# A scan, an FFN and a mixture of experts on one core: the scan's products of a chunk in one TensorE group, and PSUM split three, three and two

## The chip, the cores and the metric

One core of a Trainium2 chip runs the whole kernel. The metric is device time in microseconds (us): the median of three runs before is 608.58 us (608.17 to 608.62).

## The reference

Three stages follow one another. First a linear recurrence over 4 sequences of 768 tokens, 8 heads of 32 columns with a state of 16 (`_attn_ref`); the kernel takes it in chunks of 128 tokens. Its output, 3072 tokens of 256 columns, goes through a feed-forward layer whose activation is a rational function (`_moe_ref`), and that through a top-1 mixture of 8 experts (`_moe2_ref`).

```python
# first stage, per chunk
y_intra = einsum('bhij,bhjd->bhid', (C @ B^T) * L, x)       # L: decays, causal
y_inter = einsum('bhin,bhnd->bhid', C, state) * decay_to_i
state = decay_full * state + sum(B * x * decay_from_j)
# second stage
h = x @ w_in                                                # 256 -> 2048
g = (a0 + a1*h + a2*h^2 + a3*h^3) / (1 + |b0|*|h| + |b1|*h^2 + 1e-6)
x = g @ w_out                                               # 2048 -> 256
# third stage, for the tokens of each expert e
xn = x / (norm(x) + 1e-6);  logits = xn @ en.T / tau;  e = argmax(logits)
out = max(softmax(logits)) * (relu(x @ w1[e]) @ w2[e])      # 256 -> 1024 -> 256
```

## The kernel before

The kernel is recorded as operations with a due time `at`, an engine, a cost and the tiles that each reads and writes. `Plan.run` lists them by these: on a free engine it starts the ready operation of the earliest due time for whose new tiles there are buffers. The list fixes the order of instructions on every engine; on the chip each engine works through its list in that order and waits by semaphores.

The 3072 tokens are 24 chunks of 128 and 6 *units* of 512 (numbered 0 to 5). Work that is in the trace at the same time:

- **First stage** (`s1_chunk`, L635 to L723). For each chunk: `c` (L666), two score products, one for each half of the heads, in float32, each into a bank of its own; ScalarE and GpSimd, or VectorE, mask them into `m` (L672, L675, L680). `st` (L688): the chunk's addition to the state, which VectorE adds up in `sx` (L695, L697). `y` (L706 and L712): the outputs, made from the state before the chunk and from `m`, one operation for each half; ScalarE and VectorE copy them out as a high and a low part, `x1h` (L722) and `x1l` (L723). These four operations have due times of their own, so TensorE's list puts other work between them. The chunks of unit u+1 are made while unit u is in the second stage.
- **Second stage** (`block`, L729 to L765). Each unit has 16 blocks of 128 columns. A block's first product `h` (L738, six matmuls of 512 columns) goes to a bank of the pool `ps_h`. Five ScalarE instructions (L743, L744, L745, L749, L750), four VectorE instructions (L747, L752, L753, L754) and one GpSimd instruction (L755) work out the activation as a high and a low part, `gh` and `gl`; L754, which writes `p`, is the last that reads the bank. The second product (L764, six matmuls) adds into the two banks `acc`.
- **Routing** (`route`): after a unit the tokens are transposed with their logits (`tk`, L799, L801) and scattered to expert lists in device memory (L858).
- **Third stage**. Three short passes (`first_pass`: products `fh`, `fy`) run while the last unit ends; passes of 2 to 4 tiles of 128 tokens follow (`run_pass`). A pass loads its tokens `g` (L961), transposes them (`t`, L969), splits them into `xh` and `xl` (L972, L975), and makes the products `eh` (L1023) and `y` (L1032). `gate` (L978 to L1009) works out each token's softmax weight by a row of small instructions of VectorE and ScalarE, all on SBUF tiles. `deliver` scales the result (L1046, L1048), and GpSimd scatters it (L1052) by the token numbers in the last column of `g`.

PSUM has 8 banks. Before, 4 are in `ps_h` (for `h`, `eh`, `fh` and, at the start, weight conversions), 2 in `ps_a` (`acc`, and the third stage's `y`), 2 in `ps_s` (all that `bank()` makes: `c`, `st`, `y`, `tk`, `t` and others):

```python
H_B = 4        # banks in ps_h
S_B = 2        # banks in ps_s
```

Of the kernel before, what the change touches and what calls it, by code (L numbers as in the profile page):

```python
# [47 lines left out]
H_B = 4  # L48

DIRECT = 2  # L50
S_B = 2
# [224 lines left out]
def ssm_ffn_moe_kernel(  # L276
# [29 lines left out]
    def dve(n, k=0):  # L306
        return 0.069 + n / 960 + 0.06 * k
# [122 lines left out]
    tri, ones = keep([P, P], BF16, "tri"), keep([P, P], BF16, "ones")  # L430
    io, tok, cw8, ke, kmin = keep([P, NE], I32, "io"), keep([P, NCH], I32, "tok"), keep([P, NE], F32, "cw8"), keep([P, NE], BF16, "ke"), keep([P, NE], F32, "kmin")
# [204 lines left out]
    def s1_chunk(u, j, at, ph):  # L636
# [23 lines left out]
        ms_ = [plan.val(s1p, [P, 4, P], F32, f"m{q}{n}", "m", 3) for q in range(2)]  # L660

        def f():
# [4 lines left out]
        op("PE", 1.28, at, f, r=[t["bc"], cz], w=cs)  # L667
# [14 lines left out]
        so = state.get("s")  # L682
        if not last:
            st = bank(f"st{n}")

            def f():
                for q in range(2):
                    T.matmul(out=st[64 * q:64 * q + 64, 0:P], lhsT=bw[:, q].rearrange("p n r -> p (n r)"), rhs=t["xt"]()[:, j, q * P:(q + 1) * P], start=True, stop=True)  # L688
            op("PE", 0.3, at + ph, f, r=[bw, t["xb"]], w=[st])
            sn = sx[c_ % SX]  # L690
            for q in range(2):
                def f(q=q):
                    qs = slice(64 * q, 64 * q + 64)
                    if first:
                        V.tensor_copy(out=sn[qs, q], in_=st[qs, 0:P])  # L695
                    else:
                        V.scalar_tensor_tensor(out=sn[qs, q], in0=so[qs, q], scalar=ec[qs, 1, (j + 1) * P - 1:(j + 1) * P], in1=st[qs, 0:P], op0=ALU.mult, op1=ALU.add)  # L697
                op("DVE", dve(P, 1), at + ph + 0.3, f, r=[st] + ([] if first else [ec, (so, q)]), w=[(sn, q)])
            state["s"] = sn
        y = bank(f"y{n}")  # L700

        def f(q):
            o = slice(q * P, (q + 1) * P)
            if not first:
                for r in range(4):
                    T.matmul(  # L706
                        out=y[r * HD:(r + 1) * HD, o], lhsT=so[:, q, r * HD:(r + 1) * HD], rhs=cz[:, r, cl],
                        start=True, stop=False, skip_group_check=True, tile_position=(0, r * HD),
                    )
            for r in range(4):  # L710
                h = 4 * q + r
                T.matmul(  # L712
                    out=y[r * HD:(r + 1) * HD, o], lhsT=t["xt"]()[:, j, h * HD:(h + 1) * HD], rhs=ms_[q][:, r, :],
                    start=first, stop=True, skip_group_check=True, tile_position=(0, r * HD),
                )
        for q in range(2):
            op(
                "PE", 0.3 if first else 0.5, at + (2 + q) * ph, lambda q=q: f(q),
                r=[ms_[q], t["xb"]] + ([] if first else [cz, so]), w=[(y, q)],
            )  # L720
        yv = lambda: y[:, 0:256].rearrange("p (k t) -> p k t", k=2)
        op("ACT", act(256), at + 3 * ph + 0.7, lambda: A.activation(out=x1h[:, :, xl], in_=yv(), func=AF.Copy), r=[y], w=[(x1h, jx)])  # L722
        op("DVE", dve(256), at + 3 * ph + 0.9, lambda: V.tensor_tensor(out=x1l[:, :, xl], in0=yv(), in1=x1h[:, :, xl].bitcast(F32), op=ALU.subtract), r=[y, (x1h, jx)], w=[(x1l, jx)])  # L723
# [231 lines left out]
    def tokens(e, t0, n, at):  # L955
# [6 lines left out]
        for t in range(n):  # L962
            tr = bank(f"t3_{nm}_{t}")
            o = slice(t * P, (t + 1) * P)
# [517 lines left out]
```

## Time and profile before

| | us |
| --- | --- |
| median of 3 runs | 608.58 |
| the profiled execution | 609.72 |
| its span in the profile | 607.9 |
| TensorE busy | 555.0 (91%) |
| VectorE busy | 478.7 (79%) |
| ScalarE busy | 467.1 (77%) |
| GpSimd busy | 249.7 (41%) |

The shares are means over stages with different limits. In the times of the trace, units 0 to 5 of the second stage begin at 41, 103, 165, 228, 286 and 350 us; the last ends at 418 us, and the passes after the short ones run from 459 to 595 us. A busy TensorE is modelled from the matmuls' starts; where it shows no idle time, it may still lose time between groups of matmuls, which is read from their starts.

### The profile page before, as it was taken

What the parts mean: (1) busy time and instruction counts of PE and PEld (TensorE: products, weight loads), DVE (VectorE), ACT (ScalarE), POOL (GpSimd) and SP (SyncE); (2) the same over time, 40 slices, a digit from 0 to 9 for tenths busy, and PEclk for the clock granted to TensorE, in tenths of its full rate; (3) what the DMA queues carried; (4) which work ended last, traced back from release to release, by engine and by line L of the source; (5) the groups of instructions that cost most, each with busy time, mean ns of one, the idle gap of its engine ahead of it and who ended that gap; (6) DMA issues with size and microseconds to landing.
All of it is one profiled execution on the core that took longest, in us unless ns stands there. A gap on an engine that the chain in (4) does not pass through costs nothing.

```text
span 607.9 us, 10415 instructions
## 1 busy us (share of the span) xinstructions
PE 555.0 (91%) x3429; PEld 430.0 (71%) x3429; DVE 478.7 (79%) x989; ACT 467.1 (77%) x941; POOL 249.7 (41%) x233
## 2 busy tenths in 40 slices
PE   1667989999999999999999999899998979999991
PEld 0244657776667666767676787677888979999991
DVE  7997899989888798899997889884456667767430
ACT  6898989999998899989997998893256667557330
POOL 2573334446444444454445434433433543222111
PEclk9997999999999999999999999999999989999996
DMA  7960515113102120110010001681266855544000
GB/s 245 390 206 18 160 30 160 45 55 97 45 0 84 51 61 19 54 62 18 2 46 27 1 2 54 219 286 36 89 193 174 238 154 177 173 142 153 18 23 14
DMA packets 47919, 61.08 MB, mean 100 GB/s; under 512 B 4135, under 2 KB 37776, under 8 KB 47856
## 3 DMA queue, kind: packets, MB, share of 16 engines
q1 hardware_dynamic: 45360, 53.92, 29.0%
q0 software_dynamic: 2496, 6.41, 2.9%
q8 instruction: 29, 0.48, 0.4%
q14 instruction: 34, 0.28, 0.1%
HBM read 46.11 MB, written 14.72 MB: 100 GB/s over the span
## 4 chain that ended last, share of the span: by engine, by line
PE 59%; issue 8%; DMA 7%; DVE 7%; ACT 4%; POOL 3%; SPq 1%; another core or an unknown queue 0%; POOLq 0%; ACTq 0%
PE h L738 19%; PE acc L764 19%; PE eh L1023 4%; PE y L1032 4%; PE c L666 3%; DMA g<-xs 2%; PE y L706 2%; PE y L712 2%; DMA ra<-in_w 2%; POOL out_dram L1052 1%; PE tk L801 1%; PE fy L1119 1%; DMA out_dram<-yo,g 1%; DMA fa<-in_w 1%; DVE gh L752 1%
## 5 line engine op out<-in xcount | busy, mean ns | idle before, releaser
L755 POOL TENSOR_TENSOR gl<-p,v 128x512 fp32r<-128x512 f32 x96 | 127.4, 1329 | 176.0 <-DVE p L754 76.1
L738 PE MATMUL h<-x1h,wiw 128*128 128x512 f32 x384 | 142.0, 413 | 7.5 <-DVE p L754 5.2
L764 PE MATMUL acc<-gh,wow 128*128 128x512 f32 x384 | 112.0, 413 | 0.0
L738 PEld LDWEIGHTS h<-x1h,wiw 128*128 128x128 f32 x384 | 73.5, 192 | 34.0 <-issue 7.6
L764 PEld LDWEIGHTS acc<-gh,wow 128*128 128x128 f32 x384 | 68.0, 188 | 29.6 <-issue 15.9
L752 DVE SCALAR_TENSOR_TENSOR gh<-h,as,v 128x512 fp32r<-128x512 f32 x96 | 71.7, 747 | 14.1 <-ACT v L750 13.5
L753 DVE SCALAR_TENSOR_TENSOR u<-u,lq,gh 128x512 f32<-128x512 f32 x96 | 78.9, 822 | 0.8
L747 DVE SCALAR_TENSOR_TENSOR h<-p,sl,h 128x512 f32<-128x512 f32 x96 | 71.9, 749 | 6.7 <-ACT v L744 6.4
L738 PE MATMUL h<-x1l,wiw 128*128 128x512 f32 x192 | 76.8, 400 | 0.0
L743 ACT ACTIVATE p<-h,kk 128x512 f32<-128x512 f32 x96 | 65.3, 680 | 11.8 <-POOL gl L755 6.1
L754 DVE SCALAR_TENSOR_TENSOR p<-h,as,u 128x512 f32<-128x512 f32 x96 | 71.6, 745 | 3.0 <-DVE bw L651 0.2
L745 ACT ACTIVATE u<-v,qb 128x512 f32<-128x512 f32 x96 | 69.5, 724 | 1.5
L749 ACT ACTIVATE v<-u,lq 128x512 f32<-128x512 f32 x96 | 69.4, 722 | 1.6
L750 ACT ACTIVATE v<-v 128x512 f32<-128x512 f32 x96 | 60.4, 630 | 1.0
L764 PE MATMUL acc<-gl,wow 128*128 128x512 f32 x192 | 60.6, 396 | 0.1
L744 ACT ACTIVATE v<-h 128x512 f32<-128x512 f32 x96 | 56.9, 593 | 2.5 <-POOL gl L755 2.5
L1026 DVE SCALAR_TENSOR_TENSOR hl<-eh,hh 128x256 fp32r<-128x256 f32 (+1 forms) x72 | 34.2, 479 | 27.3 <-ACT hh L1025 26.8
L1025 ACT ACTIVATE hh<-eh 128x256 fp32r<-128x256 f32 (+1 forms) x72 | 30.5, 425 | 28.2 <-PE eh L1023 24.4
L1052 POOL DMA_INDIRECT out_dram<-yo,g x22 | 23.8, 1080 | 67.8 <-DVE yo L1048 34.6
L1032 PE MATMUL y<-ebh,hh 128*128 128x256 f32 x176 | 51.2, 291 | 0.3 <-ACT hh L1025 0.3
L1032 PE MATMUL y<-ebh,hl 128*128 128x256 f32 x176 | 50.5, 287 | 0.2 <-DVE hl L1026 0.2
L1032 PE MATMUL y<-ebl,hh 128*128 128x256 f32 x176 | 49.8, 283 | 0.0
(238 smaller groups left out, 1143.1 us busy)
## 6 DMA issues: line engine op xcount, KB each, us to landing
ra<-in_w SPq DMA_DIRECT2D x32, 256.0 KB
rb<-in_w SPq DMA_DIRECT2D x32, 256.0 KB
xb<-in_xb SPq DMA_DIRECT2D x12, 384.0 KB
xs<-empty SPq DMA_DIRECT2D x8, 530.0 KB
wiwr<-in_w_in SPq DMA_DIRECT2D x8, 512.0 KB
wowr<-in_w_out SPq DMA_DIRECT2D x8, 512.0 KB
xrow<-row SPq DMA_DIRECT2D x6, 530.0 KB
bc<-in_bct SPq DMA_DIRECT2D x12, 256.0 KB
```

What stands on the lines that cost most here:

```text
L738: T.matmul(out=h.t, lhsT=part(wiw[g_], z)[:, k, fs], rhs=xx[:, k, :], start=(k == 0 and e == 0), stop=(k == 1 and e == 2))
L743: op("ACT", act(512, 1), s, lambda: A.activation(out=pp.t, in_=h.t, func=AF.Square, bias=kk.t), r=[h, kk], w=[pp])
L745: op("ACT", acts(512) + 0.06, s + 0.3, lambda: A.activation(out=uu.t, in_=vv.t, func=AF.Square, bias=qb.t), r=[vv, qb], w=[uu])
L747: op("DVE", dve(512, 1), s + 0.8, lambda: stt(out=h.t, in0=pp.t, scalar=sl.t, in1=h.t, op0=ALU.add, op1=ALU.mult), r=[h, pp, sl], w=[h])
L749: op("ACT", acts(512) + 0.09, s + 0.9, lambda: A.activation(out=vv.t, in_=uu.t, func=AF.Ln, bias=lq.t), r=[uu, lq], w=[vv])
L750: op("ACT", acts(512), s + 1.0, lambda: A.activation(out=vv.t, in_=vv.t, func=AF.Exp, scale=-1.0), r=[vv], w=[vv])
L752: op("DVE", dve(512, 1), s + 1.5, lambda: stt(out=gh.t, in0=h.t, scalar=as_.t, in1=vv.t, op0=ALU.add, op1=ALU.mult), r=[h, as_, vv], w=[gh])
L753: op("DVE", dve(512, 1), s + 1.6, lambda: stt(out=uu.t, in0=uu.t, scalar=lq.t, in1=gh.t.bitcast(F32), op0=ALU.add, op1=ALU.mult), r=[uu, l ...
L754: op("DVE", dve(512, 1), s + 1.7, lambda: stt(out=pp.t, in0=h.t, scalar=as_.t, in1=uu.t, op0=ALU.add, op1=ALU.subtract), r=[h, as_, uu], w ...
L755: op("POOL", pool2(512), s + 2.1, lambda: G.tensor_tensor(out=gl.t, in0=pp.t, in1=vv.t, op=ALU.mult), r=[pp, vv], w=[gl])
L764: T.matmul(out=acc[dh].t, lhsT=part(wow[g_], z)[:, i % 2, dh * P:(dh + 1) * P], rhs=x.t, skip_group_check=True, start=(i == 0 and e == 0), ...
L1032: T.matmul(out=y[t // 2][:, t % 2 * DM:(t % 2 + 1) * DM], lhsT=hx[:, o], rhs=wb[w][:, f % 2, :], start=(f == 0 and i == 0 and t % 2 == 0), ...
```

## The change

1. `H_B` goes from 4 to 3 and `S_B` from 2 to 3.
2. From the second 512 tokens on (first-stage units of 256 tokens numbered 2 and up: chunks 4 to 23) a chunk's scores, its `st` and the *previous* chunk's `y` are one TensorE operation. `st` and the previous `y` share one bank `gy`. The last chunk of each 512 tokens has its `y` in an operation of its own behind that.
3. `tokens`: two tiles are transposed into one bank and copied out by one instruction each of ScalarE and VectorE.
4. `gate`: the maximum with 1e-36 becomes a bias of the logarithm, and, except in the first short pass, the small values stand in a bank of `ps_h` (`gp`).
5. GpSimd copies the token numbers out of `g` into `ix`, and the scatter reads that.
6. In the very last pass each of the two tiles has an output bank, and each tile's second product is an operation of its own.

```diff
-H_B = 4
+H_B = 3
-S_B = 2
+S_B = 3
...
+        together = u >= 2
+        pend = state.pop("pend", None)
+        if together:
+            both = bank(f"gy{n}")
+            st = both
...
+        if together:
+            def f():
+                scores()
+                if not last:
+                    states(256)
+                if pend:
+                    for q in range(2):
+                        pend[0](both, q)
+            op(
+                "PE", 0.95 + (0 if last else 0.2) + (0.45 if pend else 0), at, f,
+                r=[t["bc"], cz] + ([] if last else [bw, t["xb"]]) + (pend[1](0) + pend[1](1) if pend else []),
+                w=cs + ([] if last else [(both, 2)]) + ([(both, 0), (both, 1)] if pend else []),
+            )
+            if pend:
+                pend[2](both, at + 0.7)
+        else:
+            op("PE", 1.28, at, scores, r=[t["bc"], cz], w=cs)
...
+        if together and jx < BU // P - 1:
+            state["pend"] = sums, reads, outputs
+        elif together:
+            y = bank(f"y{n}")
...
-        for t in range(n):
+        for t in range(0, n, 2):
+            m = min(2, n - t)
...
-        dv(0.08, lambda: V.tensor_scalar(out=s2[:, 0:n], in0=s2[:, 0:n], scalar1=1e-36, scalar2=None, op0=ALU.max), [s2], [s2])
+        plan.op("ACT", 0.1, sh(at, -0.09, 0), lambda: A.activation(out=s(), in_=s2[:, 0:n], func=AF.Ln, bias=tiny.t), r=[s2, *tiny_], w=[S])
-        dv(0.08, lambda: V.tensor_tensor(out=rc[:, 0:n], in0=rc[:, 0:n], in1=s2[:, 0:n], op=ALU.mult), [rc, s2], [rc])
+            gp = plan.val(ps_h, [P, 512], F32, f"gp{nm}", "h", H_B, True)
+        dv(0.08, lambda: V.tensor_tensor(out=rc(), in0=rc(), in1=s2[:, 0:n], op=ALU.mult), [RC, s2], [RC])
...
+        for t in range(n):
+            op("PE", 1.4 / 4, sh(at + 0.8, 0.36, 0) + (6.0 if t == n - 1 and f > 4 else 0.0), lambda t=t: mm2([t], 1), r=[hh, hl, *wb], w=[y[t]])
...
-                    out=out, out_offset=bass.IndirectOffsetOnAxis(ap=g[:, t, ROW - 1:].bitcast(I32), axis=0), in_=yo.t, in_offset=None,
+                    out=out, out_offset=bass.IndirectOffsetOnAxis(ap=ix[:, t:t + 1], axis=0), in_=yo.t, in_offset=None,
...
+        ix = plan.val(sp, [P, TPE], I32, f"ix{nm}", "ix", 4)
+        op("POOL", 0.15, at + 2 * parts[0] - 2.0, lambda n=sum(parts): G.tensor_copy(out=ix[:, 0:n], in_=g[:, 0:n, ROW - 1].bitcast(I32)), r=[g], w=[ix])
```

The order on TensorE in unit 2, before: the products of chunk 13 (`c0_13` and `c1_13` are its scores; rows of other work are left out).

```order
L666 MATMUL c0_13_2080<-cz_6_1618,bc_6_1426 128x512
L666 MATMUL c1_13_2081<-cz_6_1618,bc_6_1426 128x512
...
L688 MATMUL st_13_2191<-xb_6_1180,bw_13_1716 64x128 x2
L738 MATMUL h_2_7_2194<-x1h4_1368,wiw3_470 128x512
...
L706 MATMUL y_13_2210<-cz_6_1618,sx0_132 32x128 x4
L712 MATMUL y_13_2210<-m0_13_2097,xb_6_1180 32x128 x4
L764 MATMUL acc2_0_2041<-gh_2_4_2146,wow2_453 128x512
...
L706 MATMUL y_13_2210<-cz_6_1618,sx0_132 32x128 x4
L712 MATMUL y_13_2210<-m1_13_2099,xb_6_1180 32x128 x4
```

And of the change, a little later: chunk 14's scores and `st`, and with them the `y` of chunk 13 (the rows that read `m0_13` and `m1_13`), follow one another with nothing between.

```order
L678 MATMUL c0_14_2229<-cz_7_1782,bc_7_1696 128x512
L678 MATMUL c1_14_2230<-cz_7_1782,bc_7_1696 128x512
L682 MATMUL gy_14_2231<-xb_7_1606,bw_14_1857 64x128 x2
L688 MATMUL gy_14_2231<-cz_6_1620,sx0_133 32x128 x4
L694 MATMUL gy_14_2231<-m0_13_2081,xb_6_1154 32x128 x4
L688 MATMUL gy_14_2231<-cz_6_1620,sx0_133 32x128 x4
L694 MATMUL gy_14_2231<-m1_13_2083,xb_6_1154 32x128 x4
```

So four groups between large products have become one. In TensorE's whole list such groups, each with large products (`h` or `acc`) on both sides, number 18, 19, 18 and 18 in units 1 to 4 before (the `tk` and `rk` of routing with them), and 9, 8, 8 and 7 now; in unit 0 they go from 15 to 8.

The order on VectorE in the third stage, before: the gate of the pass of expert rank 4 (`rc4_0`, `sq4_0`, `s24_0` are its small tiles) stands ahead of the splits `xl4_0` of that pass's tokens.

```order
L997 RECIPROCAL rc4_0_5626<-sq4_0_5596 128x3
L998 TENSOR_TENSOR rc4_0_5626<-rc4_0_5626,s24_0_5534 128x3
L999 TENSOR_TENSOR sq4_0_5596<-sq4_0_5596,rc4_0_5626 128x3
L1000 TENSOR_SCALAR sq4_0_5596<-sq4_0_5596 128x3
L1001 RECIPROCAL rc4_0_5626<-sq4_0_5596 128x3
L1026 SCALAR_TENSOR_TENSOR hl2_2_4_5647<-eh2_2_4_5613,hh2_2_4_5635 128x256
L975 TENSOR_TENSOR xl4_0_5652<-t3_4_0_0_5631,xh4_0_5644 128x2x128
```

And of the change (`gp4_0` is the bank with the small values, `hl4_0` an operand of that pass's second product).

```order
L1019 TENSOR_TENSOR xl4_0_5627<-t3_4_0_0_5597,xh4_0_5614 128x2x256
...
L1019 TENSOR_TENSOR xl4_0_5627<-t3_4_0_2_5629,xh4_0_5614 128x2x128
...
L1081 SCALAR_TENSOR_TENSOR hl4_0_5_5888<-eh4_0_5_5840,hh4_0_5_5875 128x384
L1019 TENSOR_TENSOR xl5_0_5892<-t3_5_0_0_5870,xh5_0_5890 128x2x256
L1052 RECIPROCAL gp4_0_5903<-sq4_0_5499 128x3
L1053 TENSOR_TENSOR gp4_0_5903<-gp4_0_5903,s24_0_5411 128x3
```

The gate has moved behind both splits and most of the pass, and its multiplication reads one operand from PSUM.

## Rows read from the trace of the kernel before

**Rows 1.** Windows: stretch and its length, then busy us (instructions) of each engine, granted TensorE clock, DMA share, GB/s.
```profile
41.20:103.27 62.07, 56.27 (x310) 37.77 (x311) 55.62 (x98) 56.37 (x106) 26.36 (x22) 0.95 0.28 81
103.27:165.27 62.00, 62.00 (x385) 43.55 (x384) 55.62 (x98) 58.98 (x108) 29.80 (x26) 1.00 0.27 76
103.27:349.87 246.60, 245.27 (x1491) 170.48 (x1490) 220.20 (x374) 227.65 (x408) 115.86 (x101) 1.00 0.15 45
349.87:417.70 67.83, 63.83 (x293) 50.36 (x292) 59.57 (x126) 58.26 (x118) 29.76 (x26) 1.00 0.40 129
458.57:595.24 136.67, 132.58 (x1002) 131.02 (x1000) 87.43 (x218) 77.28 (x202) 39.28 (x34) 0.99 0.45 137
480.00:500.00 20.00, 16.44 (x122) 15.88 (x121) 12.35 (x30) 11.33 (x34) 10.03 (x8) 0.91 0.65 193
```

**Rows 2.** The chain that ended last, 212 to 221 us: start, us, what it was.
```profile
213.40 1.06 PE c L666 x4
214.45 1.60 PE h L738 x6
216.06 0.37 PE st L688 x4
216.42 1.60 PE acc L764 x6
218.02 1.40 PE h L738 x6
219.42 0.35 PE y L706 x8
219.78 0.22 PE y L712 x8
```

**Rows 3.** Waits of ScalarE, 103 to 350 us: total us, times, longest.
```profile
ACT p L743 <- PE h L738: 5.5, 11, 1.0
```

**Rows 4.** Timeline of TensorE: first matmul of blocks 0 and 12, units 0 and 5.
```profile
41.20 0.77 PE L738 MATMUL h<-x1h,wiw 128*128 128x512 f32 x1 [1.81 <-ACT wow L571]
...
88.59 0.50 PE L738 MATMUL h<-x1h,wiw 128*128 128x512 f32 x1 [1.44 <-DVE p L754]
...
349.87 0.39 PE L738 MATMUL h<-x1h,wiw 128*128 128x512 f32 x1
...
389.74 0.50 PE L738 MATMUL h<-x1h,wiw 128*128 128x512 f32 x1 [0.83 <-DVE p L754]
```

**Rows 5.** Timeline of VectorE: `p` of those blocks; the third is unit 2, block 13.
```profile
53.86 0.73 DVE L754 SCALAR_TENSOR_TENSOR p<-h,as,u 128x512 f32<-128x512 f32 x1
...
100.47 0.75 DVE L754 SCALAR_TENSOR_TENSOR p<-h,as,u 128x512 f32<-128x512 f32 x1
...
226.19 0.75 DVE L754 SCALAR_TENSOR_TENSOR p<-h,as,u 128x512 f32<-128x512 f32 x1
...
357.96 0.75 DVE L754 SCALAR_TENSOR_TENSOR p<-h,as,u 128x512 f32<-128x512 f32 x1
...
403.45 0.75 DVE L754 SCALAR_TENSOR_TENSOR p<-h,as,u 128x512 f32<-128x512 f32 x1
```

**Rows 6.** Timeline of all engines, 490 to 494.5 us.
```profile
490.18 2.93 DVE L998 TENSOR_TENSOR rc<-rc,s 128x3 f32<-128x3 f32 x1
...
490.59 1.28 POOL L950 TENSOR_TENSOR eal<-ra,eah 128x512 fp32r<-128x512 f32 x1
...
491.80 1.27 POOL L950 TENSOR_TENSOR ebl<-rb,ebh 128x512 fp32r<-128x512 f32 x1
...
494.41 0.33 PE L969 MATMUL t<-ident,g 128*128 128x128 f32 x1 [3.56 <-DVE xl L975]
```

**Rows 7.** Waits of TensorE, 400 to 480 us: total us, times, longest.
```profile
PE ck L1181 <- DVE xl L975: 1.4, 1, 1.4
PE tk L799 <- ACT row L804: 1.2, 1, 1.2
```

**Rows 8.** Timeline of GpSimd, from 590 us: the last scatter.
```profile
597.32 0.97 POOL L1052 DMA_INDIRECT out_dram<-yo,g  x1 [0.30 <-issue]
```

More of the change, by code (lines that the diff above doesn't have):

```diff
@@ L660, in s1_chunk, with scores @@
         ms_ = [plan.val(s1p, [P, 4, P], F32, f"m{q}{n}", "m", 3) for q in range(2)]
-        def f():
+        so = state.get("s")
+        together = u >= 2
+        pend = state.pop("pend", None)
+        st = y = None
+        if together:
+            both = bank(f"gy{n}")
+            st = both
+        elif not last:
+            st = bank(f"st{n}")
+        def scores():
             for q in range(2):
@@ L681, in s1_chunk @@
                 op("DVE", dve(512), at + 0.3, g, r=[c, mask], w=[m])
-        so = state.get("s")
         if not last:
[L684 to L689, printed above, removed]
+            so_ = 256 if together else 0
+            if not together:
+                op("PE", 0.3, at + ph, lambda: states(0), r=[bw, t["xb"]], w=[st])
             sn = sx[c_ % SX]
@@ L699, in s1_chunk @@
+                op("DVE", dve(P, 1), at + ph + 0.3, f, r=[(st, 2) if together else st] + ([] if first else [ec, (so, q)]), w=[(sn, q)])
             state["s"] = sn
[L700 to L723, printed above, removed]
+        if together and jx < BU // P - 1:
+            state["pend"] = sums, reads, outputs
+        elif together:
+            y = bank(f"y{n}")
+            def f():
+                for q in range(2):
+                    sums(y, q)
+            op("PE", 0.75, at + 2.5 * ph, f, r=reads(0) + reads(1), w=[(y, 0), (y, 1)])
+            outputs(y, at + 3 * ph + 0.7)
+        else:
+            y = bank(f"y{n}")
+            for q in range(2):
+                op("PE", 0.3 if first else 0.5, at + (2 + q) * ph, lambda q=q: sums(y, q), r=reads(q), w=[(y, q)])
+            outputs(y, at + 3 * ph + 0.7)
@@ L1066, in run_pass @@
             nm = f"{e}_{t0 + q}"
[L1067 removed]
+            per = 1 if apart and q + n == sum(parts) else 2
+            y = [plan.val(*z, True) for z in [(ps_a, [P, 512], F32, f"y{nm}_{b}", "acc", 2) for b in range((n + per - 1) // per)]]
             for f in range(8):
[L1069 removed]
+                hidden(nm, e, q, n, f, xh, xl, y, at + f * n / 4, per == 1)
             at += 2 * n
[L1071 removed]
+            deliver(nm, q, n, ix, y, gt, at + 0.9, per)
             q += n
@@ L1098, in first_pass @@
         op("ACT", act(2 * n * P), at - 1.5, lambda: A.activation(out=x.t.rearrange("p k t -> p (k t)"), in_=tr[:, 0:2 * n * P], func=AF.Copy), r=[tr], w=[x])
-        gt = gate(plan, nm, g, n, at + 4 * step, blk)
+        gt = gate(plan, nm, g, n, at + 4 * step, blk, not small, [tiny])
+        ix = plan.val(blk, [P, 2], I32, f"fix{nm}", "fix", 3)
+        op("POOL", 0.15, at + 4 * step, lambda: G.tensor_copy(out=ix[:, 0:n], in_=g[:, 0:n, ROW - 1].bitcast(I32)), r=[g], w=[ix])
         y = bank(f"fy{nm}") if small else plan.val(ps_a, [P, 512], F32, f"fy{nm}", "acc", 2, True)
```

122 lines of the change are left out of this document (76 added, 46 removed).

## The prediction

> **What bounds the kernel now.** I read the windows by stage first. While units 1 to 4 are in the second stage (103.27 to 349.87 us) TensorE is busy for 245.27 of 246.60 us; in the passes from 458.57 us on for 132.58 of 136.67 [rows 1]. So in both stretches time is won only where TensorE has less to do, or where it no longer stands still. The reader should also see what comes next: ScalarE is busy for 227.65 us of the first stretch (92.3%), and in its densest part, unit 1, for 58.98 of 62.00 us (95.1%). VectorE stands at 220.20 us (89.3%).
>
> Busy time hides what the change is about, so I then followed the chain that ended last, which is TensorE work end to end. A large product takes 1.40 us behind another large one and 1.60 us behind one of the first stage's groups; the groups themselves take 1.06 (`c`), 0.37 (`st`) and 0.35 + 0.22 us (half of `y`) [rows 2]. A group that stands alone therefore costs its own time and 0.20 us more.
>
> Last I looked at what limits a bank of `ps_h`: from a block's first matmul to the end of its `p`. Block 13 of unit 2 starts at 218.02 in the chain and its `p` ends at 226.94, which is 8.9 us [rows 2, 5]. A block comes every 3.9 us there (62.00 / 16, [rows 1]), so three banks give 11.6 us. In units 0 and 5 it is longer: over blocks 0 to 12 of unit 0 the first takes 13.4 us and the last 12.6, with a mean of 14.1 over the 13; in unit 5 the first takes 8.8 and the last 14.5, mean 12.7 [rows 4, 5].
>
> **The change, part by part.**
>
> *One group per chunk, units 1 to 4.* The order counts 73 groups between large products before and 32 after, 41 fewer. At 0.20 us [rows 2] that is 8.2 us. Inside a merged group each product may also lose some of the start that it pays alone. No row shows one at full clock, so I bound it by nothing and by 0.25 us for each of 16 chunks (4 us), and take 0.1 us, since the rows that read `m` take only 0.22 us behind rows of the same kind against 0.35 us for the first of a pair [rows 2]. TensorE would then need 9.8 us less. Not all of that can arrive. ScalarE's 227.65 us at the 95.1% it reached in unit 1 make 239.4 us, 7.2 less than 246.6. **I take 7.** The bounds are 2 (ScalarE at 93%, 244.8 us) and 12 (TensorE alone). For ScalarE's rising share speaks that 5.5 us of its idle time here is waiting for a first product [rows 3].
>
> The Trainium skill speaks against a part of this: its page "TensorEngine Tiling (Array Packing)", section "Key Properties", says that a change of tiling mode drains TensorE, and inside a merged group the mode still changes, from `c` to `st` to `y`. If each of the two changes around a lone group costs 0.1 us, 146 changes become some 90, and TensorE saves 5.6 us in place of 9.8.
>
> *What the merged group waits for.* It now needs the scores' inputs, `bw` and the masks of the previous chunk at once; behind it stand a large product and everything that TensorE has. All of these are old by then: in the order of units 1 to 4 at least three large products lie between a group and the one that its masks come from. A chunk's `y` comes one group later, but a unit's last `y` now stands ahead of block 11's first product, where it stood behind block 14's, so `x1h` and `x1l` of the next unit are not later. I cost it at nothing; should the two copies of `c` be late, ScalarE is the cover that has gone.
>
> *Unit 0.* Seven groups fewer, 1.4 us, but TensorE is not the bound: 56.27 busy of 62.07 us, ScalarE 56.37, VectorE 55.62 [rows 1]. Fewer banks may cost: if 14.1 us stayed, three banks would give a block every 4.7 us; it is 3.95 now (12 blocks from 41.20 to 88.59, [rows 4]), so 12 blocks lose 9.1 us. Bounds -2 and +9. I take 0: the 14 us are mostly queueing behind the blocks ahead, and fewer blocks in flight shorten it towards the 8.9 us of unit 2.
>
> *Unit 5.* There TensorE runs ahead at 3.3 us a block (349.87 to 389.74, [rows 4]) while ScalarE and VectorE are busy for 58.26 and 59.57 of 67.83 us [rows 1]. Three banks stop it earlier. Bounds 0 and +11 (12.7 / 3 is 4.2 us, 0.9 more for 12 blocks); **I take +1**, since the end of the unit hangs on the vector chain, and short passes fill TensorE behind it.
>
> *The gate.* On VectorE one tiny multiplication of two SBUF tiles takes 2.93 us, from 490.18 to 493.11, while GpSimd runs two subtractions from 490.59 to 493.07; the splits behind it are late, and TensorE waits 3.56 us for a bank of `t` [rows 6]. That wait is followed by a low clock: granted 0.91 over 20 us [rows 1], so 1.8 us lost at the lower of its two levels (1.2 of 2.4 GHz). In the new order the splits stand ahead of the gate, and `ix` lets the next `g` be loaded before the scatter is done. **I take -5** of 5.4; bounds 0 and -5.4.
>
> The Trainium skill, "SBUF — State Buffer", section "SBUF: two separate sides", says that VectorE with two SBUF inputs and GpSimd lock each other out for a whole instruction. The 2.93 us row agrees; by that page the multiplication would not wait even where it stood, since one operand is now in PSUM.
>
> *Two more waits of TensorE:* 1.2 us of `tk` for a small bank and 1.4 us before `ck` for the first split [rows 7]. A third small bank, and tokens freed earlier by `ix`, may take both: bounds 0 and -2.6; **I take -1.5**.
>
> *The tail.* The last tile's scatter ends the kernel, behind that of the tile ahead of it, which takes 0.97 us and 0.30 us of issue [rows 8]. In the order the two tiles still alternate, so the earlier tile gains only half of the last block's second product. Bounds 0 and -1.3; **I take -0.4**.
>
> *The rest at nothing:* fewer copies of tokens and the dropped maximum lie beside TensorE. Eleven small GpSimd copies lie on an engine busy for 39.28 of 136.67 us [rows 1]; a copy that waits for its `g` holds the scatters and weight subtractions queued behind it, and only if the tokens were later than those would TensorE see it. The gate's bank leaves two of three to `eh`, and a block there uses one for less time than two products take.
>
> **The sum:** -7 + 0 + 1 - 5 - 1.5 - 0.4 = -12.9 us, so 596.8 for an execution like the profiled one (609.72). That one was 1.1 us above the median of 608.58, so against the median: **595.7 us**.
>
> **The rivals.**
>
> *A. Three banks are too few (slower).* A wait of the first product for `p` takes the place of what was saved. It decides if a bank's 14.1 and 12.7 us in units 0 and 5 do not shrink: that is when they exceed three periods, 11.8 us in unit 0 and 10.0 in unit 5. Price: 9.1 + 11.0 = 20.1 us, less the 13.9 won elsewhere: +6.2, so 614.8 us. For it: first products already wait for `p` there with four banks, 1.44 and 0.83 us [rows 4]. Against it: with less queueing a block needs 8.9 us. Chance 0.13.
>
> *B. ScalarE is the bound already.* Units 1 to 4 win 2 us and not 7: 600.7 us. For it: 92.3% on average. Against it: 95.1% in unit 1, with TensorE the one that was late. Chance 0.16.
>
> *C. Changing between small products costs as much as going back to large ones.* At 0.1 us for each of the 146 changes before and some 90 after, TensorE saves 5.6 us, and that is what units 1 to 4 win: 597.1 us. For it: `c` and `st` are followed by the same 0.20 us, though one is three times as long [rows 2]. Against it: the two parts of a `y` follow each other with no such time. Chance 0.08. This is what the Trainium skill's "TensorEngine Tiling (Array Packing)", section "Key Properties", would make of it.
>
> *D. Half of A.* Banks cost about 13 us and what is won is given back: 608.6 us. Chance 0.05.
>
> The forecast itself has 0.58.
>
> **How the numbers follow.** About 0.2%, 1.2 us, is what a measurement of this kernel can tell from no change. The forecast, B and C are faster by more: 0.82. D is the same: 0.05. A is slower: 0.13. The lower end, 586, is units 1 to 4 at 12, and the other terms near their better bounds. The upper end, 605, takes in B with 4 us of bank waits; above it lie A, D and a little of B.
>
> **What would show it.** Right: in the chain a merged group of 2.5 us or less with one 1.60 us product behind it; units 1 to 4 in about 239 us with ScalarE near 95%; no TensorE wait of 3.56 us near the third stage's `t`, and a granted clock of 1.00 there; units 0 and 5 no longer than 62 and 69 us. Wrong: rows of `h` waiting for `p` that sum to more than 10 us (A); ScalarE at 93% with TensorE waiting for it (B); a merged group of over 2.6 us (C). If VectorE turned out to be the engine that limits units 1 to 4, the sum would be wrong in a way that none of these names.

## The result, and the profile after

The changed kernel takes **598.85 us** (median of 4 runs, 597.82 to 599.36), the kernel before, run beside it, 608.60 (4 runs, 608.17 to 608.73): 9.75 us less, a ratio of 0.9844 with a 95% interval of 0.9803 to 0.9885. The forecast was 595.7 us (586 to 605), and faster. The total came near. How it comes about is not how the prediction had it: alone, the first stage's part won nothing and the third stage's part won 15.5 us, as e1 and e2 below show.

The profiled execution of the changed kernel took 597.82 us with a span of 596.1, 11.8 us less than the span before. Its windows by stage (stretch, length, then busy us and instructions of PE, PEld, DVE, ACT and POOL, granted clock, DMA share, GB/s): unit 0, units 1 to 4, unit 5 to the last `acc`, the short passes, the passes to the last `y`, the end.

```profile
44.07:105.92 61.85, 55.51 (x324) 38.47 (x324) 57.57 (x97) 57.70 (x110) 25.28 (x22) 0.95 0.35 100
105.92:347.91 241.99, 233.37 (x1479) 169.90 (x1477) 214.28 (x369) 224.87 (x401) 111.31 (x100) 1.00 0.14 39
347.91:419.82 71.91, 65.08 (x294) 50.44 (x295) 60.70 (x107) 59.58 (x116) 33.12 (x29) 1.00 0.40 126
419.82:454.61 34.79, 34.79 (x187) 30.45 (x186) 16.72 (x55) 14.66 (x37) 15.67 (x16) 1.00 0.47 145
454.61:585.48 130.87, 130.87 (x1006) 130.43 (x1004) 86.02 (x236) 76.79 (x199) 42.09 (x41) 1.00 0.47 139
585.48:596.10 10.62, 0.00 (x1) 0.00 (x0) 0.17 (x1) 0.47 (x1) 1.94 (x2) 0.69 0.07 20
```

In units 1 to 4 TensorE is busy for 11.9 us less than in [rows 1], but the stretch is only 4.6 us shorter: TensorE's idle time has grown from 1.3 to 8.6 us, and ScalarE is busy for 92.9%. From 419.82 us on TensorE has no idle time until the last `y`, at a granted clock of 1.00.

The two stretches do not hold quite the same work. With three banks the first products run ahead of the second ones by a block less, and one second product, one chunk's scores and one `st` that stood in units 1 to 4 before now stand in unit 0: between the first `h` of units 1 and 5 there are 390 matmuls of `acc` and 64 of `c` before, 384 and 60 now. By [rows 2] that is 1.40 + 1.06 + 0.37 = 2.8 us of TensorE. Like stands beside like from the first `h` of all to unit 5: 308.67 us before, 303.84 now, 4.8 less.

The same stages of every profile, in us (each sums to the span; `first h` is the time before unit 0). The lengths repeat well where the lists are the same: units 1 to 4 take 243.45, 243.49 and 243.47 us in e2, e6 and e7, and 246.60 and 246.63 before and in e5. One does not fit: e9, with the lists of e2 on TensorE and, as shown below, its pace, takes 2.0 us less than e2. It ran on another chip than e2, e6 and e7; why it differs is open.

| | first `h` | unit 0 | units 1 to 4 | unit 5 | short passes | passes | end | span |
| --- | --- | --- | --- | --- | --- | --- | --- | --- |
| before | 41.20 | 62.07 | 246.60 | 68.39 | 40.31 | 136.67 | 12.66 | 607.9 |
| changed | 44.07 | 61.85 | 241.99 | 71.91 | 34.79 | 130.87 | 10.62 | 596.1 |
| e1 first stage only | 44.92 | 62.66 | 243.90 | 72.31 | 35.97 | 134.08 | 12.86 | 606.7 |
| e2 third stage only | 41.31 | 60.78 | 243.45 | 68.68 | 34.79 | 130.87 | 10.52 | 590.4 |
| e3 no groups | 45.43 | 60.25 | 239.91 | 70.64 | 34.79 | 130.99 | 10.59 | 592.6 |
| e4 conversions | 39.09 | 68.49 | 241.13 | 71.02 | 34.79 | 130.87 | 10.51 | 595.9 |
| e5 = e2, no `ix` | 41.20 | 60.89 | 246.63 | 67.17 | 43.89 | 133.54 | 10.48 | 603.8 |
| e6 = e2, gate in SBUF | 41.17 | 60.77 | 243.49 | 70.77 | 36.47 | 133.43 | 10.60 | 596.7 |
| e7 = e2, single tokens | 41.14 | 60.68 | 243.47 | 68.82 | 35.65 | 130.38 | 10.46 | 590.6 |
| e8 half groups, 4 and 2 | 41.21 | 58.51 | 238.36 | 71.22 | 34.78 | 130.88 | 10.44 | 585.4 |
| e9 = before, pad | 41.19 | 60.79 | 241.45 | 69.71 | 39.36 | 134.88 | 12.22 | 599.6 |
| e10 = changed, pad | 44.93 | 62.90 | 240.70 | 70.93 | 34.79 | 130.63 | 10.52 | 595.4 |
| e11 half groups, 3 and 3 | 44.12 | 61.46 | 237.27 | 71.38 | 34.79 | 130.92 | 10.46 | 590.4 |
| e12 four masks | 44.35 | 61.82 | 241.38 | 71.16 | 34.79 | 130.87 | 10.53 | 594.9 |

TensorE's timeline of the changed kernel in unit 4 (start, us, line, out<-in, in brackets the idle time ahead and what ended it): a merged group and the two first products behind it.

```profile
318.19 1.13 PE L678 MATMUL c<-cz,bc 64*128 64x512 f32 x4
...
320.30 0.40 PE L694 MATMUL gy<-m,xb 128*32 128x128 f32 x8
320.63 0.50 PE L779 MATMUL h<-x1h,wiw 128*128 128x512 f32 x1
...
322.60 0.50 PE L779 MATMUL h<-x1h,wiw 128*128 128x512 f32 x1 [0.31 <-DVE p L795]
```

From 318.19 to 320.63 the group holds TensorE for 2.44 us. Two first products stand in a row behind it, and the second has to wait for a bank. The chain shows the price of a large product, as [rows 2] did: here 1.58 us behind a group, 1.36 behind another large one.

```profile
134.53 1.36 PE acc L805 x6
...
145.19 0.22 PE gy L694 x8
145.41 1.58 PE acc L805 x6
```

Waits from 105.92 to 347.91 us (engine, line, what was waited for: us in total, times, longest):

```profile
PE h L779 <- DVE p L795: 6.3, 12, 1.3
ACT p L784 <- PE h L779: 5.2, 11, 1.2
DVE m L734 <- PE gy L694: 2.8, 4, 1.0
```

First products now wait for `p`, that is for one of the three banks; no such row stands in this stretch before. Over the whole kernel they sum to 13.2 us. ScalarE's wait for `h` is not new: it was 5.5 us before [rows 3].

At the start the first four chunks are done by 33.9 us, and then TensorE waits 10.16 us for a bank that a weight conversion holds:

```profile
43.25 0.68 DVE L549 SCALAR_TENSOR_TENSOR go<-wowr,bo 128x512 int32<-128x512 int32 x1
...
44.07 0.77 PE L779 MATMUL h<-x1h,wiw 128*128 128x512 f32 x1 [10.16 <-ACT fo L545]
```

The conversion's last reader of its bank `bo` ends at 43.93 us, and the first `h` starts 0.14 us later. Banks are handed out by due time, so the first `h` comes when all conversions ahead of it but two have given theirs back; with four banks it was all but three.

In the third stage the gate's multiplication on VectorE (L1053) stands between the splits and takes 0.16 us, where it took 2.93 [rows 6]. GpSimd is at a subtraction of the weights beside it:

```profile
486.49 0.16 DVE L1052 RECIPROCAL gp<-sq 128x2 f32<-128x2 f32 x1
486.63 0.69 DVE L1019 TENSOR_TENSOR xl<-t,xh 128x512 fp32r<-128x512 f32 x1
487.24 0.16 DVE L1053 TENSOR_TENSOR gp<-gp,s 128x2 f32<-128x2 f32 x1
...
487.24 1.29 POOL L991 TENSOR_TENSOR eal<-ra,eah 128x512 fp32r<-128x512 f32 x1
```

### The profile page after: what moved, and what is told of

It reads as the page before. It is cut to its first block, busy times and chain, and to the rows that moved or that the text cites. A ratio compares the mean times of both kernels' runs of the same rounds, so it can differ in the third digit from the quotient of the medians.

```text
span 596.1 us, 10428 instructions
## 1 busy us (share of the span) xinstructions
PE 535.3 (90%) x3429; PEld 425.4 (71%) x3429; DVE 474.5 (80%) x970; ACT 468.7 (79%) x930; POOL 251.6 (42%) x246
## 4 chain that ended last, share of the span: by engine, by line
PE 51%; ACT 18%; DVE 10%; issue 7%; DMA 2%; SPq 1%; POOL 1%; POOLq 0%; ACTq 0%; DVEq 0%
PE eh L1078 9%; PE h L779 9%; PE acc L805 9%; PE y L1087 9%; ACT p L784 4%; PE fy L1185 3%; PE fh L1175 3%; ACT u L786 3%; ACT v L785 3%; ACT v L790 3%; DVE u L794 3%; ACT v L791 2%; PE c L678 2%; DVE p L795 2%; DVE gh L793 2%
## 5 line engine op out<-in xcount | busy, mean ns | idle before, releaser
L779 PE MATMUL h<-x1h,wiw 128*128 128x512 f32 x384 | 142.8, 413 | 25.8 <-DVE p L795 13.2
L805 PE MATMUL acc<-gh,wow 128*128 128x512 f32 x384 | 106.1, 398 | 0.0
L805 PEld LDWEIGHTS acc<-gh,wow 128*128 128x128 f32 x384 | 70.7, 188 | 15.0 <-issue 1.0
L794 DVE SCALAR_TENSOR_TENSOR u<-u,lq,gh 128x512 f32<-128x512 f32 x96 | 80.6, 840 | 0.5
L805 PE MATMUL acc<-gl,wow 128*128 128x512 f32 x192 | 59.3, 390 | 0.2 <-POOL gl L796 0.2
L1112 POOL DMA_INDIRECT out_dram<-yo,ix x22 | 23.0, 1048 | 53.9 <-DVE yo L1108 37.7
```

The costliest lines, as they stand in the source:

```text
L779: T.matmul(out=h.t, lhsT=part(wiw[g_], z)[:, k, fs], rhs=xx[:, k, :], start=(k == 0 and e == 0), stop=(k == 1 and e == 2))
L794: op("DVE", dve(512, 1), s + 1.6, lambda: stt(out=uu.t, in0=uu.t, scalar=lq.t, in1=gh.t.bitcast(F32), op0=ALU.add, op1=ALU.mult), r=[uu, l ...
L805: T.matmul(out=acc[dh].t, lhsT=part(wow[g_], z)[:, i % 2, dh * P:(dh + 1) * P], rhs=x.t, skip_group_check=True, start=(i == 0 and e == 0), ...
```

## The experiments

Kernels that ran together on one chip, each set beside runs of before: e1 to e4 (before 607.6 us), e5 to e8 (606.1), e9 to e11 (602.9), e12 (606.2). The time of before moves by more from set to set than it did within the first one, so times are compared inside a set, and between sets by the stages above, which are those of one execution each. The changed kernel itself ran in none of these sets; e4, e10 and e12 are nearest to it.

**e1, the first stage's part alone.** The third stage's functions are those of before.

```diff
 H_B = 3
 S_B = 3
-        run_pass(e, t0, parts, at, j == len(FIRST + THEN) - 1)
+        run_pass(e, t0, parts, at)
```

> The 3/3 split of the banks and the merged groups alone, with the third stage as before. Theory (the first stage's groups and the third stage are two separate gains): the start keeps its loss of 2.9 us (first h at about 44.1 us), units 1 to 4 take 242 us, unit 5 loses some 2 to 3.5 us, and the passes from the first eh to the last y take 135 to 137 us with the 3.56 us wait for xl in them: 608 to 611 us in all, so no gain. Rival (the gain of the third stage comes from the third small bank or from an earlier start of it): those passes take 133 us or less, and the time is 603 us or less.

Measured: 607.8 us against 607.58, ratio 0.9994 (0.9971 to 1.0018). No gain, as the theory has it. On before, units 1 to 4 win 2.7 us, the short passes 4.3 and the passes 2.6 (a little more than the theory allowed, less than the rival wanted); the late first `h` costs 3.7 and unit 5 3.9. From 107.58 to 351.48 us, units 1 to 4:

```profile
107.58:351.48 243.90, 236.58 (x1478) 170.10 (x1477) 213.64 (x369) 224.89 (x400) 111.26 (x100) 1.00 0.13 39
```

**e2, the third stage's part alone.** Banks 4 and 2, first stage of before.

```diff
 H_B = 4
 S_B = 2
-        run_pass(e, t0, parts, at)
+        run_pass(e, t0, parts, at, j == len(FIRST + THEN) - 1)
```

> Before, with the third stage's edits alone (tokens two at a time, gate in PSUM, token numbers copied, last pass apart), banks 4 and 2, no merged groups. Theory: first h at 41.2 us, units 1 to 4 in 246 to 247 us, passes in about 131 us without the 3.56 us wait: 600 to 603 us. Rival (the third stage needs the third small bank): waits of TensorE for t or tk stay, 605 us or more.

Measured: **592.05 us** against 607.58, ratio 0.9749 (0.9710 to 0.9787), 15.5 us less and beyond the range of either theory. The short passes (-5.5) and the passes (-5.8) are as short as in the changed kernel. Units 0 to 4 are 4.4 us shorter too, with the lists of before on every engine but for one tiny GpSimd write; nothing that the edits compute explains that (e9 and e10).

**e3, the change without merged groups.**

```diff
-        together = u >= 2
+        together = False
```

> The changed kernel without the merged groups: banks 3 and 3, third stage as changed. Theory (the groups cost TensorE 0.2 us each, three banks cost only the start and unit 5): units 1 to 4 in 246 to 248 us, total 603 to 605 us. Rival (three banks already cost several us in units 1 to 4, and the merged groups win that back and more): units 1 to 4 in 250 us or more, 607 us or more in all.

Measured: 594.97 us, ratio 0.9799 (0.9761 to 0.9837), and beyond both theories. It is 3.5 us less than e4 in the same set, which is the changed kernel but for the banks of four conversions; the slowest run here (595.86) is below the fastest there (597.59).

```profile
105.68:345.59 239.91, 238.51 (x1481) 168.51 (x1480) 217.65 (x369) 227.25 (x403) 114.59 (x100) 1.00 0.13 39
```

```profile
PE h L779 <- DVE p L795: 0.6, 3, 0.2
```

TensorE is busy for 5.1 us more than with merged groups, with as many second products and scores in the stretch, and the stretch is 2.1 us shorter, because it waits 0.6 us for banks in place of 6.3. Three small banks alone already bring the groups from 73 to 63. Against e2 in the same set, the banks cost 2.9 us, 2.2 of them in the spans: 4.1 at the start and 2.0 in unit 5, less 0.5 in unit 0 and 3.5 in units 1 to 4 (which hold 2.8 us less work with three banks).

**e4, other banks for the last conversions.**

```diff
-        bk = plan.val(ps_h, [P, 2, 256], F32, "b" + n, "h", H_B, True)
+        bk = bank("b" + n, (P, 2, 256)) if n in ("o4", "o5", "o6", "o7") else plan.val(ps_h, [P, 2, 256], F32, "b" + n, "h", H_B, True)
```

> The changed kernel with the last four conversions of the output weights in banks of ps_s in place of ps_h. Theory (the first h starts late because the conversions ahead of it hold the three banks): first h at 41 us or earlier, and the end comes 2 to 3 us earlier, 596 to 597 us. Rival (ScalarE, which has the conversions to do, sets the end of unit 0 anyway): first h earlier, unit 0 longer by the same, unit 1 still begins at about 106 us and the time stays at 598 to 599 us.

Measured: 598.49 us, ratio 0.9860 (0.9821 to 0.9900). The first `h` does come at 39.09 us, so the conversions' banks were what it waited for; but unit 1 begins at 107.58, 1.7 later than in the changed kernel, and nothing is left of the gain. The rival's outcome, though its reason is not shown: in unit 0 ScalarE has 6.0 us of idle time (4.2 in the changed kernel), and the granted clock is 0.86 over 68.49 us, so 9.6 us are lost at the lower level, against 3.1 at 0.95. The difference is about what unit 0 is longer by.

```profile
39.09:107.58 68.49, 59.74 (x324) 40.72 (x325) 61.29 (x106) 62.52 (x116) 30.02 (x26) 0.86 0.32 97
```

**e5, e2 without the copy of the token numbers.** The copies and their tiles `ix` go with the edit shown.

```diff
-                    out=out, out_offset=bass.IndirectOffsetOnAxis(ap=ix[:, t:t + 1], axis=0), in_=yo.t, in_offset=None,
+                    out=out, out_offset=bass.IndirectOffsetOnAxis(ap=g[:, t, ROW - 1:].bitcast(I32), axis=0), in_=yo.t, in_offset=None,
```

> The third-stage edits alone (as e2, 592.1 us), with the scatter reading the token numbers from g again. Theory (the copy of the numbers lets the tokens be loaded earlier and makes the last scatter cheaper to issue or land): from the last scatter's start to the end of the span 10.5 us again where e2 has 8.8, and one or two waits of TensorE for tokens in the passes: 594 to 597 us. Rival (the copy is worth nothing, the gain is the gate's and the last pass's): 592 us and 8.8 us at the end.

Measured: 605.91 us against 606.13, ratio 0.9989 (0.9962 to 1.0017). Without `ix` the whole gain of e2 is gone, more than the theory expected; the long end of the span (10.48 here) did not come back, so that is not the copy's. Units 1 to 4 are at 246.63 us again, with unchanged lists (e9 and e10); the most is lost in the short passes (the second row is the part of them at the low clock, the third a wait of TensorE ahead of it):

```profile
415.89:459.78 43.89, 40.74 (x187) 34.37 (x186) 14.51 (x46) 13.77 (x35) 10.58 (x11) 0.88 0.34 110
421.00:431.20 10.20, 10.20 (x35) 8.68 (x35) 0.72 (x3) 1.56 (x4) 1.26 (x1) 0.50 0.00 0
```

```profile
PE tk L801 <- ACT x2T L778: 1.8, 2, 1.6
```

They take 9.1 us more than in e2. 3.2 us are idle time of TensorE, and at a granted clock of 0.88 some 5.3 of 43.89 us are lost at the lower level. None of this waits for tokens. Without `ix` the plan also lists TensorE's short passes in another order (four matmuls of `fh` now stand ahead of the first `tk`, and at that `tk` TensorE stands still), so how much of the 9.1 us is the tile that stays held, and how much the other order and the clock, is not shown. What `ix` does to the loads is seen on the queue of SP. Before, the load of the fourth pass's tokens goes out at 480.75 us, after a scatter that starts at 476.85, and its transposes start at 488.59; in the changed kernel it goes out at 464.20, 20 us ahead of its transposes (484.48). First before, then the change:

```profile
480.75 0.37 SPq L961 DMA_DIRECT2D g<-xs  x1
```

```profile
464.20 0.37 SPq L1002 DMA_DIRECT2D g<-xs  x1
```

**e6, e2 with the gate's values in SBUF.**

```diff
-        gt = gate(plan, nm, g, sum(parts), at + 2 * parts[0] - 2.0, sp, True, [tiny])
+        gt = gate(plan, nm, g, sum(parts), at + 2 * parts[0] - 2.0, sp, False, [tiny])
-        gt = gate(plan, nm, g, n, at + 4 * step, blk, not small, [tiny])
+        gt = gate(plan, nm, g, n, at + 4 * step, blk, False, [tiny])
```

> The third-stage edits alone (as e2, 592.1 us), with the gate's small values in SBUF as before. Theory (tiny VectorE instructions with two SBUF operands are held up behind GpSimd's subtractions of the weights, and the splits of the tokens behind them are late): several such rows of 1.3 to 2.9 us, TensorE waits of 2 us or more in the passes, a granted clock under 1.00 there, 597 to 602 us. Rival (only the order mattered: splits ahead of the gate): no TensorE wait of over 1 us, 592 to 594 us.

Measured: 598.49 us, ratio 0.9882 (0.9848 to 0.9916); its span is 6.3 us longer than e2's. The time is the theory's, the signs are the rival's: of long rows there is one, no wait in the passes is over 1 us, and the clock stays at 1.00. The loss is spread (unit 5 +2.1, short passes +1.7, passes +2.6). The plan also lists TensorE in another order in the short passes, and VectorE in unit 5: there two instructions of a short pass's gate now stand ahead of a block's `h`, and VectorE waits 2.59 us for that pass's tokens, more than unit 5 is longer by. So the 6.3 us are not the price of the gate's place in SBUF alone.

```profile
391.23 0.17 DVE L1018 TENSOR_REDUCE mx<-fg 128x2 f32<-128x16 f32 x1 [2.59 <-DMA fg<-xs]
...
472.45 1.98 DVE L1014 TENSOR_TENSOR rc<-rc,s 128x3 f32<-128x3 f32 x1
```

```profile
472.10 0.98 POOL L1073 DMA_INDIRECT out_dram<-yo,ix  x1 [0.30 <-DVE eal L952]
473.10 1.30 POOL L952 TENSOR_TENSOR eal<-ra,eah 128x512 fp32r<-128x512 f32 x1
```

The multiplication of two SBUF tiles begins beside a scatter and ends at 474.43, just as the subtraction behind that scatter does on GpSimd, at 474.40. With one operand in PSUM it took 0.16 us beside such a subtraction. The Trainium skill, "SBUF — State Buffer", section "SBUF: two separate sides", has it that VectorE with two SBUF inputs and GpSimd lock each other out for a whole instruction. The trace agrees (1.98 us against 0.16); that the multiplication, which began first, waited for the end of the subtraction too is more than the sentence says.

**e7, e2 with tokens one tile at a time** (`tokens` as before).

```diff
-        for t in range(0, n, 2):
+        for t in range(n):
```

> The third-stage edits alone (as e2, 592.1 us), with the tokens transposed and copied one tile at a time as before. Theory (the pairs lie beside TensorE's work and are worth nothing): 592 to 593 us. Rival (with two small banks the four transposes of a pass wait for a bank, and pairs remove that): waits of TensorE for t, 594 us or more.

Measured: 593.90 us, ratio 0.9808 (0.9777 to 0.9839), between the theory's 593 and the rival's 594. Its span is 0.2 us longer than e2's, TensorE has no idle time in the passes, and the ratios of the two sets overlap: the pairs are worth nothing that shows.

**e8, half the grouping, banks 4 and 2.** The scores are an operation of their own.

```diff
             def f():
-                scores()
                 if not last:
                     states(256)
...
+            op("PE", 1.0, at, scores, r=[t["bc"], cz], w=cs)
...
-H_B = 3
+H_B = 4
-S_B = 3
+S_B = 2
```

> The third-stage edits with banks 4 and 2, and half of the grouping: the scores of a chunk stand alone, st and the previous y are one group in one bank (e2, 592.1 us, has no groups). Theory (what cost time in the full grouping is that 2.4 us of small products stand in one piece, and the banks): TensorE's shorter list counts, units 1 to 4 in 240 to 242 us and 589 to 591 us in all. Rival (any grouping starves ScalarE and VectorE of first products or delays y): units 1 to 4 in 244 us or more, 593 us or more.

Measured: **588.26 us**, ratio 0.9718 (0.9684 to 0.9752): 2.8% less than before, the shortest time of all runs here and a little under the theory's 589 to 591. It is 5.6 us less than e7 of the same set, which has neither groups nor pairs. Units 1 to 4 take 238.36 us, 5.1 less than in e2 with the same work in them.

```profile
99.72:338.08 238.36, 236.42 (x1491) 171.16 (x1490) 216.66 (x375) 223.73 (x409) 114.05 (x102) 1.00 0.14 43
```

```profile
PE h L780 <- DVE p L796: 1.2, 4, 0.4
```

**e9 and e10, the place of the tiles.** A small tile that nothing reads moves the second stage's weights in SBUF, away from the tiles that they are multiplied with. In e9 (before) it has 3 buffers, which move them by 96 bytes, as the change does; in e10 (the changed kernel) one, in the first short pass only, which makes the 96 bytes 128.

```diff
+        pad = plan.val(blk, [P, 2], I32, f"pad{nm}", "pad", 3)
+        op("POOL", 0.0, at + 4 * step, lambda: G.memset(pad.t, 0), r=[g], w=[pad], port=False)
```

> The kernel before with one edit that computes nothing: a small tile with three buffers (96 bytes of a partition) is taken from blk, as ix does in the change, so that the weights of the second stage lie 96 bytes further in SBUF from the tiles that they are multiplied with; the lists of all engines are those of before, but for three tiny GpSimd writes near 390 us. In the profiles so far the products of 512 columns follow one another in 231 to 232 ns in the kernels whose weights lie as before (before, e1, e5) and in 227 to 228 ns in those with 96 bytes more (the change, e2, e3, e4, e6, e7, e8). Theory (the place of the tiles sets the pace of the products): 227 to 228 ns, first h to unit 5 in 304 to 305 us in place of 308.7, and 602 to 604 us in all. Rival (something else in the third-stage edits sets it): 231 ns, 308 us, 606 to 608 us.

> The changed kernel with 32 bytes more in blk, so that the weights lie 128 bytes further from those tiles than before, in place of 96; lists as in the changed kernel, but for one tiny GpSimd write near 390 us. If the pace of the products goes by the distance in steps of 64 bytes (32 left over: slow, as before; none left over: fast, as in the change), 128 bytes bring back 231 to 232 ns and cost 3 to 4 us: 602 to 603 us. Rival (any shift away from the place of before does, or the place does not matter): 227 ns and 598 to 599 us.

Measured: e9 601.94 us against 602.91, ratio 0.9976 (0.9940 to 1.0012); e10 597.91, ratio 0.9919 (0.9890 to 0.9948). The pace of the products turned both ways as the theory says; the times did not follow it (e10's 597.91 us is the rival's 598 to 599). The chain of e9, a kernel of lists as before, now shows 1.36 us for a large product behind a large one, where [rows 2] has 1.40:

```profile
206.26 1.58 PE h L738 x6
207.85 1.36 PE acc L764 x6
```

and that of e10, lists of the changed kernel, shows 1.40 in place of 1.36:

```profile
129.41 1.40 PE h L779 x6
130.81 1.40 PE acc L805 x6
```

What it is worth in the end is not settled. e9's first `h` to unit 5 takes 302.24 us, 6.4 less than in the profile of before, but its median is not measurably below that of before in its own set, of which there is no profile. In e10 the same stretch takes 303.60 us, the changed kernel's 303.84, at a slower pace of TensorE: with merged groups that pace did not show in the time.

**e11, half the grouping, banks 3 and 3** (the scores taken out of the changed kernel's group, as in e8).

```diff
-                scores()
...
+            op("PE", 1.0, at, scores, r=[t["bc"], cz], w=cs)
```

> The changed kernel with the scores of a chunk taken out of the merged group into an operation of their own, due at the same time; st and the previous y stay one group, due a little later. Banks 3 and 3. e8, the same with banks 4 and 2, took 588.3 us. Theory (the scores in the group cost most, because the masks wait for more of the group and every other user of a small bank waits for three free ones; the banks cost what e3 against e2 shows, 3 us): 590 to 592 us. Rival (the banks cost most once the groups are merged): 595 us or more.

Measured: 595.17 us against 602.91, ratio 0.9885 (0.9830 to 0.9940), 2.7 us less than e10 in the same set; the median lies where the rival has it, so three banks cost more beside groups than the theory said. The profiled execution was the fastest of the four (592.12). By its stages, taking the scores out wins 5.7 us on the changed kernel, 4.7 of it in units 1 to 4, and the banks cost 5.0 us against e8 (start 2.9, unit 0 3.0, less 1.1 in units 1 to 4); by the medians both are less certain.

```profile
PE h L780 <- DVE p L796: 1.8, 4, 0.5
```

**e12, four mask buffers in the changed kernel.**

```diff
-        ms_ = [plan.val(s1p, [P, 4, P], F32, f"m{q}{n}", "m", 3) for q in range(2)]
+        ms_ = [plan.val(s1p, [P, 4, P], F32, f"m{q}{n}", "m", 4) for q in range(2)]
```

> The changed kernel with four mask buffers m in place of three. In the merged group the y of a chunk is made behind the scores of the next, so the masks of both are wanted at once, four tiles; with three the mask of VectorE waits for the first half of y in the same group (in the change 2.8 us of VectorE idle over 4 rows of m, one of them with 1.0 us of TensorE behind it). Theory (this wait is what the merged group costs): no row of m waits for gy, and units 0 to 5 from the first h to unit 5 in 299 to 301 us in place of 303.8, 594 to 596 us. Rival (the group costs by holding TensorE for 2.4 us in one piece, so that first products come late and then in a row until a bank is missing): the rows of h that wait for p stay at 5 us or more, 303 us, and 598 to 599 us.

Measured: 598.46 us against 606.21, ratio 0.9870 (0.9836 to 0.9903). No mask waits for `gy` any more, and it changes nothing: from the first `h` to unit 5 303.20 us. The theory falls, the rival holds:

```profile
PE h L779 <- DVE p L795: 6.4, 12, 1.3
```

Together with e3, e8 and e11: in units 1 to 4, pieces of small products (runs of them with no large product between) longer than 2 us number 13 in the changed kernel and e12, 2 in e11, none in e3 and e8; first products wait 6.3, 6.4, 1.8, 0.6 and 1.2 us for a bank (e8 has four banks, the others three).

## Why the prediction was right in its total, and where it was wrong

The total is right by luck: two errors cancel. The terms of the first two stages, with the start, were to bring -6 us and brought +1.6; those of the third stage were to bring -6.9 and brought -13.3. The table goes by the two profiles, which lie 11.8 us apart where the medians lie 9.75: the profiled execution was 1.1 us above the median before and 1.0 below it after.

| term | predicted | in the profile |
| --- | --- | --- |
| start (not in the sum) | 0 | +2.9 |
| unit 0 | 0 | -0.2 |
| units 1 to 4 | -7 | -4.6 |
| unit 5 | +1 | +3.5 |
| `tk`, `ck` (short passes) | -1.5 | -5.5 |
| gate (passes) | -5 | -5.8 |
| tail | -0.4 | -2.0 |
| sum | -12.9 | -11.8 |

*One group per chunk.* Two steps failed. The first is the size of what TensorE saves. Where the pace is that of before, its busy time in units 1 to 4 falls by 8.7 us (236.58 us in e1, 245.27 in [rows 1]), but 2.8 of these are the work that now stands in unit 0. That leaves 5.9 us for 41 groups, 0.14 each, where the prediction took 0.20 from one place of the chain, added 1.6 and had 9.8. Rival C's count gave 5.6; but its sign, a merged group of over 2.6 us, did not come (2.44), so why a group was worth less is open. The Trainium skill's page "TensorEngine Tiling (Array Packing)", section "Key Properties", says that a change of tiling mode drains TensorE; no run here sets such a drain apart from the rest.

The second step is "What the merged group waits for ... I cost it at nothing". It asked what the group waits for, and not what is held up while it runs. Behind 2.4 us in one piece first products come in a row: of the 64 times from one block's first product to the next in units 1 to 4, 34 are under 3.2 us in the changed kernel and 18 in e3, by the starts in the records; the means are 3.8 and 3.7. At the end of unit 4 the period is 3.1 us (341.62 to 344.71), and a block that holds its bank for 9.2 us takes three of those. The cover was thin besides: the 8.9 us that the prediction read for a bank were one block, and a short one. The mean of units 1 to 4 was 10.4 us before, with 12 of 64 blocks over the 11.6 us that three banks give; now it is 10.3, with 17. ScalarE waits for `h` for 5.2 us, against 2.8 in e3 but 5.5 before, so that it is worse off than before is not shown.

So idle time replaced the saving: the merged groups are a loss of 2.1 us in units 1 to 4 against e3, which has the same banks and the same place of the weights. From the first `h` to unit 5 the changed kernel is 4.8 us shorter than before. e2 is 4.4 and e9 6.4 shorter there without a merged group, and e1, with merged groups and the weights in their old place, 2.1. The place of the weights alone may account for what was won.

The signs that the prediction set up for its rivals A and B both appeared: waits of `h` for `p` of over 10 us, and ScalarE at 93% with TensorE waiting. What they cost was made up for by the third stage.

*The start.* "The rest at nothing" forgot a user of `ps_h`: the weight conversions, though [rows 4] names one as the releaser of the first `h`. It is 2.9 us late. e4 shows that to start it earlier gains nothing by itself, and e3 that the delay can be made up by unit 5.

*Unit 5* lost 3.5 us where 1 was taken, inside the bounds. e3 against e2 puts 2.0 on the banks; e8 with four banks also takes 2.5 more than e2 there, so the rest is not the banks' alone, and open.

*The two waits of TensorE* are gone, and the term was too small because it priced the waits alone. With the idle time of 2.6 us went a granted clock of 0.96 over 40 us, which is 1.6 more; 1.3 remain that no row names. The stretch is 4.3 us shorter in e1, with the third small bank and without `ix`, and 5.5 in e2, with `ix` and two small banks: either way serves, and the parts do not add up.

*The gate* is right in size, with the step that failed in what stands beside it: the prediction had the new order and `ix` as helpers of this one term. By the spans, putting the gate back into SBUF costs 6.3 us (e6 against e2), and taking out `ix` 13.4 (e5 against e2): 9.1 in the short passes, where e5 is 3.6 us slower than even the kernel before, 2.7 in the passes, 3.2 in units 1 to 4, where it does nothing but move the weights, less 1.5 in unit 5. Both edits also change the order of the lists (for 2.1 of the 6.3 us, those of unit 5, a row names it), so these are prices in this plan, and what a held tile or the gate's place costs by itself stays open.

*The tail.* Until the last scatter starts, 0.36 us were won (1.72 us behind the last product; before, 2.08), as predicted. Another 1.7 lie between that start and the end. They are there in every profile with the new last pass and in none with the old; by e5, e6 and e7 it is not `ix`, the gate or the pairs, and the last pass was not tried alone.

## What to carry to other kernels

Merging small products takes work from the engine that runs them, but it also makes a longer piece: before merging, look at the longest piece and at the period of the blocks just behind it, not at the mean, and read the hold of a buffer from all blocks, not from one. Price an idle gap of TensorE with the clock that follows, and look for a buffer that a late reader holds: leaving out eleven small copies cost 13.4 us here, part of it through other orders and places that came with them. Before a difference of two stretches is read as a saving, count the work in both. And when a sum comes out right, undo the parts one at a time before believing it: this change holds a loss, and its better half alone, or with half of the grouping, is the faster kernel.

## What the runs showed of the hardware

- Identical lists ran at two paces: six matmuls of 512 columns in 1.36 or 1.40 us; by the starts in the records the matmuls mostly follow each other in 226 to 227 ns, or in 231 to 235. A tile of 96 or 32 bytes that nothing reads turned one into the other (e9, e10). In the kernels seen, 1.36 goes with weights that lie 96 bytes further from the tiles they are multiplied with than before, 1.40 with the distance of before and with 128 bytes more. Why that distance matters was not tried, and what it is worth in time is not settled.
- In e5 a wait of TensorE of 1.6 us was followed by 10.20 us at the lower level of its clock (0.50 granted), which cost more than the wait: 5.1 us.
- A tiny VectorE instruction on two SBUF tiles ended with the GpSimd instruction beside it, after 1.98 us in e6 and 2.93 before, and took 0.16 beside GpSimd with one operand in PSUM.
